# Attention beside a spectral mix: folded scans earlier, sums on another engine, two spectral blocks at another place

## The chip, the core and the metric

The kernel runs on one core of a Trainium2 chip. The time is the device time of one execution in microseconds (us), as the median of several runs. TensorE (PE) multiplies matrices into PSUM, VectorE (DVE) and ScalarE (ACT) read PSUM, GpSimd (POOL) works on SBUF, SyncE (SP) issues most transfers (DMAs). "PEld" in the profile is PE's loading of weights, which overlaps with its matmuls.

## What is computed

Two results over 2048 rows of 512 columns are mixed by a gate per row.

```python
g = sigmoid((x * gate_w).sum(-1, keepdims=True))
# a: attention, 32 heads of 16 columns
qkv = (x @ wqkv) split into q, k, v by heads
p = softmax(q k^T * 16**-0.5);  a = (p v, heads joined) @ wo
# b: spectral part, the real part of a transform along columns, then along rows
ar = x @ dft_hid_re^T;  ai = x @ dft_hid_im^T
b = dft_seq_re @ ar - dft_seq_im @ ai
out = g * a + (1 - g) * b
```

## The kernel before, in words

Most products are taken in three parts for precision: an operand is split into a high and a low part (`hi`, `lo`), and hi x hi, hi x lo and lo x hi are summed in PSUM. `halves_of` (L180) issues one such part as a pair of matmuls, one for each half of the rows, into two PSUM banks; the two halves are added afterwards. A pair is also called a slot, because `products` (L331) calls `beside()` (L284) after each pair, and `beside()` is where other work is interleaved by hand: it runs what `after(n, f)` had put down for n slots later (`run_due`), and issues scans at a pace.

A *scan* takes the scores of 128 queries with 512 keys for the two heads of a pair of heads, and from them the maximum that the softmax will subtract. There are 16 pairs of heads and 64 scans for each, 1024 in all (`TOTAL`). A *plain* scan (`scan`, L125) is a pair of matmuls into a tile of two banks and one DVE reduction of 128x1024. A *folded* scan (`scan_folded`, L140) compares keys two by two: ACT takes relu of the scores with the difference of two key blocks, DVE adds the scores of the second block and takes the maximum of the sums in the same instruction. It needs differences of keys in DRAM (`kf_d`), which `fold_keys` (L405) prepares out of stored keys, and single banks (`psk`: d0, d1, k0, k1) instead of the two-bank tiles of `pss1`.

The program has three stages.

1. The projections (L376 to L594): `project_t` for queries and keys (32 tiles of 12 slots, stored to DRAM), then `project_s` for values, real and imaginary spectral operands (48 tiles of 12 slots): 960 slots. In `project_s` ACT copies both halves out of PSUM (L472, L473), and POOL adds them four slots later (L544, L568). The sums for the spectral operands are stored to DRAM and loaded back, and ACT and POOL split them (`split_operand`, L348). Plain scans of the first three pairs of heads run beside this stage, one in 3.9 slots from slot 192 on.
2. The spectral blocks (L599 to L694): 24 of the 32 blocks of 48 slots (16 real, 8 imaginary), 1152 slots, with coefficients that POOL splits (`prepare`). Beside them run 500 folded scans, one in 2.19 slots. At the boundary of the stages the `pss1` banks are closed and `psk` is opened (L596).
3. The attention (L959): 512 steps, each with scores, exponentials on ACT (L233, L241) and products with values (L723, `pv`). The remaining scans go one to a step with plain reductions, 332 of them; from step `MIX` = 333 on, the 8 spectral blocks that are left (`LATER`, in `spectral`, L843) and then the output projection take that place, three pairs to a step.

`FRONT` = 564 + 16 x `LATER` is the number of scans ahead of stage 3. `load_scan_beside` (L276) loads the rows of the next pair of heads with eight DMAs from ACT's queue. `shift` (L162) works up the maxima of a finished pair on DVE. What orders the work is thus the order of the calls in the program; every engine executes its own instructions in that order, and waits by semaphores.

## Time and profile before

| | us |
|---|---|
| median of 3 runs | 1741.79 |
| lowest and highest of them | 1741.0, 1744.22 |
| the profiled execution | 1744.89 |
| its span, first to last instruction | 1743.1 |
| PE, DVE, ACT, POOL busy | 1716.2, 1159.3, 1451.3, 719.3 |

The views used below are: the page's head; busy time of each engine by stretch of the span ("PE busy (x)" is busy time and number of instructions, then the granted clock as a share of full speed, the busy share of the DMA engines and GB/s); groups of instructions by line and shape ("busy, mean ns of one | idle time before them, and what ended it"); waits ("engine, what waited <- what it waited for: us in total, times, longest"); and the timeline of an engine (start, duration, engine, line, operation, and in brackets the idle time before it and what ended it). A busy PE is not PE at its peak, since matmuls overlap.

### The profile page before, as it was taken

The numbers are of one execution on the slowest core, as the hardware profiler recorded it, in microseconds if no ns is written. First come the engines' busy times: TensorE is split into PE (matmuls) and PEld (weight loads), VectorE is DVE, ScalarE is ACT, GpSimd is POOL, SyncE is SP. The second block draws the span as 40 slices with busy tenths as digits, with TensorE's granted clock in tenths as the row PEclk, the third lists the DMA queues.
The fourth block names the chain that finished last, engine by engine and source line by source line (L and its number), as shares of the span: only waits on it lengthen the run. The fifth ranks groups of instructions, "written<-read, shape, count | busy, mean of one in ns | idle before, by whom it ended". The sixth has DMA issues, their size and how long they took to land.

```text
span 1743.1 us, 35510 instructions
## 1 busy us (share of the span) xinstructions
PE 1716.2 (98%) x13640; PEld 1030.2 (59%) x13640; DVE 1159.3 (67%) x1877; ACT 1451.3 (83%) x2383; POOL 719.3 (41%) x818
## 2 busy tenths in 40 slices
PE   8999999999999999999999999999999999999998
PEld 7997777888888887333333333333334555555554
DVE  6899998999999988666666666666663212222333
ACT  5445436888888888999999999999999888888885
POOL 3688668555556664132323223232332322322222
PEclk9999999999999999999999999999999999999999
DMA  7782767343345546432332513515313254255712
GB/s 257 257 296 75 219 187 235 112 122 114 100 152 150 145 134 112 85 65 55 63 62 56 96 29 78 81 24 98 77 36 73 68 115 91 68 139 133 184 36 100
DMA packets 126777, 199.54 MB, mean 114 GB/s; under 512 B 53984, under 2 KB 56528, under 8 KB 119696
## 3 DMA queue, kind: packets, MB, share of 16 engines
q1 hardware_dynamic: 84336, 161.02, 35.0%
q0 software_dynamic: 38496, 19.47, 5.2%
q10 hardware_dynamic: 3776, 16.78, 3.7%
q8 instruction: 107, 1.75, 0.4%
q14 instruction: 62, 0.51, 0.1%
HBM read 135.14 MB, written 62.66 MB: 113 GB/s over the span
## 4 chain that ended last, share of the span: by engine, by line
PE 82%; DVE 7%; DMA 5%; POOL 2%; issue 2%; ACT 1%; SPq 0%; DVEq 0%; POOLq 0%; ACTq 0%
PE pvb L723 27%; PE s L209 18%; PE xy L184 17%; PE s L184 8%; PE s L153 7%; DVE mx L136 5%; PE s L134 5%; DMA lc<-ob 1%; DMA fa<-ks_d 1%; DMA abr<-ab_d 1%; POOL s L274 1%; DMA kf_d<-fa 1%; DMA raws<-wqkv 0%; DMA ab_d<-ab 0%; DVE fold L159 0%
## 5 line engine op out<-in xcount | busy, mean ns | idle before, releaser
L136 DVE TENSOR_REDUCE mx<-s 128x2 f32<-128x1024 f32 x524 | 627.2, 1222 | 205.0 <-PE s L134 204.9
L233 ACT ACTIVATE eb<-s 128x1024 f32<-128x1024 f32 x512 | 578.0, 1129 | 55.2 <-PE s L209 55.1
L241 ACT ACTIVATE e<-s 128x512 f32<-128x512 f32 x1022 | 607.6, 705 | 1.1 <-PE s L209 1.1
L723 PE MATMUL pvb<-eb,va 128*17 128x512 f32 x2052 | 515.9, 597 | 0.0
L723 PE MATMUL pvb<-e,va 128*17 128x512 f32 x2044 | 515.0, 597 | 0.0
L209 PEld LDWEIGHTS s<-qs,ks 50*128 50x128 f32 x2048 | 211.8, 184 | 368.0 <-ACT eb L233 280.6
L209 PE MATMUL s<-qs,ks 50*128 50x512 f32 x2048 | 427.1, 436 | 0.0
L184 PE MATMUL xy<-b,c 64*128 64x512 f32 x2640 | 420.0, 392 | 0.3 <-ACT c L340 0.3
L159 DVE CUSTOM_DVE_ANT_0 fold<-s,fold 128x512 f32<-128x512 f32 x500 | 338.4, 690 | 35.8 <-PE s L153 17.6
L157 ACT ACTIVATE fold<-s 128x512 f32<-128x512 f32 x500 | 295.7, 602 | 69.7 <-PE s L153 42.5
L184 PEld LDWEIGHTS xy<-b,c 64*128 64x128 f32 x2640 | 297.7, 187 | 16.8 <-ACT c L340 0.6
L153 PE MATMUL s<-ks,qs 48*128 48x512 f32 x1000 | 230.0, 403 | 5.8 <-DVE mx L159 5.2
L134 PE MATMUL s<-ks,qs 48*128 48x512 f32 x1048 | 214.6, 396 | 6.0 <-DVE mx L136 5.8
L735 POOL DMA_DIRECT2D lc<-ob x124 | 62.9, 514 | 299.3 <-DVE ob L732 299.1
L723 PEld LDWEIGHTS pvb<-eb,va 128*17 128x17 f32 x2052 | 69.1, 95 | 190.1 <-issue 181.9
L153 PEld LDWEIGHTS s<-ks,qs 48*128 48x128 f32 x1000 | 125.2, 184 | 45.2 <-DVE mx L159 18.0
L742 POOL DMA_DIRECT2D r_d<-lc x31 | 18.1, 583 | 295.2 <-DVE lc L741 283.8
L372 POOL TENSOR_TENSOR c<-craw,c 128x512 fp32r<-128x512 f32 x92 | 120.5, 1310 | 7.4
L371 POOL CAST c<-craw 128x512 fp32r<-128x512 f32 x92 | 56.9, 619 | 137.8 <-PE xy L184 134.2
L134 PEld LDWEIGHTS s<-ks,qs 48*128 48x128 f32 x1048 | 102.9, 183 | 17.6 <-DVE mx L136 10.6
L184 PE MATMUL xy<-w,b 64*128 64x512 f32 x768 | 105.9, 393 | 2.4 <-ACT ty L473 2.2
L744 POOL DMA_DIRECT2D rb<-r_d x124 | 60.1, 493 | 70.5 <-DMA r_d<-lc 70.5
(130 smaller groups left out, 1511.9 us busy)
## 6 DMA issues: line engine op xcount, KB each, us to landing
craw<-ci SPq DMA_DIRECT2D x64, 256.0 KB
craw<-cr SPq DMA_DIRECT2D x60, 256.0 KB
ks<-k_d SPq DMA_DIRECT2D x46, 256.0 KB
qs<-q_d SPq DMA_DIRECT2D x46, 256.0 KB
ab_d<-ab SPq DMA_DIRECT2D x32, 256.0 KB
y_d<-y SPq DMA_DIRECT2D x32, 256.0 KB
o_d<-oh POOLq DMA_DIRECT2D x28, 256.0 KB, 9.9
o_d<-ol POOLq DMA_DIRECT2D x28, 256.0 KB, 11.7
```

The lines of the kernel that those rows point to most:

```text
L134: nc.tensor.matmul(ps[:, j, :], qs[b:b + 48, qb * P:(qb + 1) * P], ks[b:b + 48, c * 512:(c + 1) * 512], start=True, stop=True)
L136: nc.vector.tensor_reduce(mx[p][:, :, qb, c], ps, axis=AX.X, op=ALU.max)
L153: nc.tensor.matmul(ps, qs[b:b + 48, qb * P:(qb + 1) * P], ks[b:b + 48, c * 512:(c + 1) * 512], start=True, stop=True)
L157: nc.scalar.activation(fold[j], ps, AF.Relu)
L159: nc.vector.tensor_tensor_reduce(out=fold[j], in0=ps, in1=fold[j], scale=1.0, scalar=-3.0e38, op0=ALU.add, op1=ALU.max, accum_out=mx[p][:, ...
L184: nc.tensor.matmul(ps[j], lhs[r], rhs[r], start=first, stop=last)
L209: nc.tensor.matmul(pss[j], ks[b:b + 50, kb * P:(kb + 1) * P], qs[b:b + 50, q0:q0 + 512], start=True, stop=True)
L233: nc.scalar.activation(e, ps, AF.Exp, scale=SCALE)
L241: nc.scalar.activation(e[j], pss[j], AF.Exp, scale=SCALE)
L372: sub(lo, raw, hi.bitcast(F32))
L723: nc.tensor.matmul(pvb[r:r + VC, :], va[:, kb, 2 * p + j, :], es[c][j], start=kb == 0, stop=kb == NB - 1, tile_position=(0, r))
L735: nc.gpsimd.dma_start(lc[32 * n:32 * n + 32, :], ob[r + DH:r + VC, :].rearrange("p (s e) -> p s e", e=16))
```

## The change

Five things are changed.

- `LATER` is 10 instead of 8: two more of the imaginary spectral blocks are computed beside the attention, and 32 more scans ahead of it (`FRONT` 724 instead of 692, `MIX` 301 instead of 333).
- Scans are folded from the second pair of heads on. The change of banks moves from the boundary of the stages into the projections (`begin_folds`), the pace of folded scans is 2.67 slots there and 2.12 behind it (2.97 at two places). `scan_plain` goes.
- The pairs of heads are scanned in another order: 0, 4, 5, 6, 7, 1, 2, 3, 8, 9, then the first 20 scans of pair 11, then 10 (`SEQ`), and rows are loaded at other points (`ROWS`). For the heads 8 to 15 (the second block of 128 columns) the key differences are taken directly from the projected keys (`difference`); `fold_keys` is left for the first and the third block.
- In `project_s` ACT copies only one half, and DVE adds the other half directly from PSUM, three slots later, for values and for spectral operands.
- The program is built with a smaller scratch for the descriptors of dynamic DMAs.

```diff
-LATER = 8
+LATER = 10
-PACE = 3.9
-FOLDED = range(3 * SCANS, FRONT)
-FOLD_PACE = 2.19
-NARROW = 5.3
+FOLDED = range(SCANS, FRONT)
+PACE, BESIDE, PART, SWAP = 3.9, 2.67, 2.12, 2.97
+PART_PAIR = FRONT // SCANS
+EARLY = [0, 4, 5, 6, 7, 1, 2, 3, 8, 9]
+SEQ = [(p, i) for p in EARLY for i in range(SCANS)]
+SEQ += [(PART_PAIR, i) for i in range(FRONT % SCANS)] + [(p, i) for p in range(len(EARLY), PART_PAIR) for i in range(SCANS)]
+SEQ += [(n // SCANS, n % SCANS) for n in range(FRONT, TOTAL)]
+ROWS = {SCANS * n + (36 if n else 40): p for n, p in enumerate(EARLY[1:])}
+ROWS.update({SCANS * len(EARLY) - 54: PART_PAIR, SCANS * len(EARLY) - 24: len(EARLY)})
...
             def beside():
...
-                pace[1] += (PACE / FOLD_PACE if seen[0] in FOLDED else 1.0) / pace[0]
-                if seen[0] == FOLDED[0] and not beds:
-                    pace[1] = 0.0
+                pace[1] += 1.0 / pace[0]
...
-                    if n % SCANS == 36 and n - n % SCANS + SCANS < FRONT:
-                        load_scan_beside(n // SCANS + 1)
+                    if n == FOLDED.start:
+                        begin_folds()
+                    if n in ROWS:
+                        load_scan_beside(ROWS[n])
                     if n not in FOLDED:
-                        done = scan_plain(n)
+                        scan(n, s1())
+                        done = n
...
+            fp = pf.enter_context(tc.tile_pool(name="fp", bufs=2, reuse_waits="tile"))
+            banks = ExitStack()
+            pss1.append(banks.enter_context(tc.tile_pool(name="pss1", bufs=2, space=PSUM)))
+
+            def begin_folds():
+
+                banks.close()
+                psk.append(ctx.enter_context(tc.tile_pool(name="psk", bufs=1, space=PSUM, reuse_waits="tile")))
+                beds.extend((lambda tag: narrow(tag, "s"), fp))
+                scan_at(BESIDE)
...
+                def difference(f, c, s):
+
+                    kept.append(s)
+                    if c % 2 == 0:
+                        return
+                    a, b = kept
+                    kept.clear()
+                    hi = ep.tile([P, 512], F32R, tag="dh", name="dh")
+                    lo = a.bitcast(F32R)
...
+                    after(11, nc.gpsimd.tensor_sub, a, a, b)
+                    after(16, nc.scalar.copy, hi, a)
+                    after(17, nc.gpsimd.tensor_sub, lo, a, hi.bitcast(F32))
+                    after(22, store, 0, hi)
+                    after(25, store, 1, lo)
...
-                    if folded and 0 < f < ND - 1:
+                    if folded and f == 1:
+                        difference(f, c, s)
+                    if folded and f == 2:
                         after(10, nc.sync.dma_start, ks_d[f][:, c * 512:(c + 1) * 512], s)
...
-                    tx = ep.tile([P, 512], F32, tag="tx", name="tx", bufs=1)
-                    ty = ep.tile([P, 512], F32, tag="ty", name="ty", bufs=3)
+                    tx = ep.tile([P, 512], F32, tag="ty", name="tx", bufs=3)
                     nc.scalar.mul(tx, ps[0], sign)
-                    nc.scalar.mul(ty, ps[1], sign)
-                    after(4, use, t, tx, ty)
+                    after(3, use, t, tx, ps[1], nc.vector.tensor_add if sign > 0 else nc.vector.tensor_sub)
...
-                def to_values(t, tx, ty):
-                    nc.gpsimd.tensor_add(va[:, t, :, 0:DH], tx.rearrange("p (h e) -> p h e", e=DH),
-                                         ty.rearrange("p (h e) -> p h e", e=DH))
+                def to_values(t, tx, ps, add):
+                    add(va[:, t, :, 0:DH], tx.rearrange("p (h e) -> p h e", e=DH),
+                        ps.rearrange("p (h e) -> p h e", e=DH))
...
-                        nc.gpsimd.tensor_add(ab, tx, ty)
-                        after(7, nc.sync.dma_start, ab_d[i][t], ab)
+                        add(ab, tx, ps)
+                        after(5, nc.sync.dma_start, ab_d[i][t], ab)
...
-                for n, wait in enumerate((18, 78, 138, 170, 202, 234)):
-                    after(wait, fold_keys, *divmod(n, 2))
+                for n, wait in enumerate((18, 78, 138, 202)):
+                    after(wait, fold_keys, 2 * (n // 2), n % 2)
...
-                    if t == 12:
-                        scan_at(5.0)
...
-    nc = bacc.Bacc("TRN2", target_bir_lowering=False, num_devices=1)
+    nc = bacc.Bacc("TRN2", target_bir_lowering=False, num_devices=1, dynamic_dma_scratch_size=4096)
```

44 lines of the change are left out of this document (16 added, 28 removed).

## The prediction

> **What bounds the kernel now.** I first read the head of the page, for the span and the share of each engine.
>
> ```profile
> span 1743.1 us, 35510 instructions
> ...
> PE 1716.2 (98%) x13640; PEld 1030.2 (59%) x13640; DVE 1159.3 (67%) x1877; ACT 1451.3 (83%) x2383; POOL 719.3 (41%) x818
> ```
>
> TensorE (PE) looks full over the whole span, so the busy share alone tells nothing about which part could become shorter. Therefore I cut the span into stretches at the marks of the program (first scan, end of the projections, first attention step, first spectral block behind the scans) and read the busy times by stretch. The bracket behind each busy time counts instructions.
>
> ```profile
> core 0: us, PE busy (x) PEld busy (x) DVE busy (x) ACT busy (x) POOL busy (x), PEclk, DMA share, GB/s
> 56.80:113.10 56.30, 56.30 (x485) 56.02 (x481) 55.08 (x49) 27.87 (x51) 43.54 (x35) 1.00 0.77 265
> 142.70:170.60 27.90, 27.90 (x242) 22.62 (x240) 27.90 (x26) 14.57 (x34) 23.63 (x20) 1.00 0.26 76
> 170.60:289.60 119.00, 113.39 (x958) 88.97 (x957) 115.03 (x108) 49.67 (x95) 82.89 (x66) 1.00 0.74 218
> 289.60:691.90 402.30, 396.55 (x3314) 341.70 (x3312) 362.27 (x1046) 329.49 (x573) 230.14 (x226) 1.00 0.47 130
> 711.38:1263.16 551.78, 550.14 (x4063) 206.00 (x4061) 372.29 (x347) 550.43 (x871) 164.63 (x248) 1.00 0.35 65
> 1331.84:1594.08 262.24, 262.24 (x2164) 139.16 (x2160) 55.84 (x96) 233.91 (x362) 69.58 (x103) 1.00 0.43 104
> ```
>
> Four things are to be seen, and matmuls come in pairs throughout, one for each half of the rows.
>
> 1. In the first two rows PE issues 485 + 242 matmuls in 56.30 + 27.90 us, so a pair costs 84.2 / 363.5 = 0.2316 us when nothing holds PE up. This is the floor.
> 2. The third row, the end of the projections, has 958 matmuls, 479 pairs, which would take 110.9 us at the floor. It took 119.0, so 8.1 us were lost. The fourth row, the spectral blocks, has 1657 pairs or 383.8 us of floor in 402.3 us: 18.5 us lost. Projections and spectral blocks are thus bounded by PE, with a loss of 5 to 7%.
> 3. In the fifth row, the attention steps with a scan each, a step has 14 matmuls (4 scores, 2 scan, 8 values), so 4063 are 290 steps of 551.78 / 290 = 1.903 us. ScalarE (ACT) is busy for 550.43 of the 551.78 us: ACT sets this pace.
> 4. In the sixth row, the steps with spectral work, a step has 18 matmuls, 2164 are 120 steps of 262.24 / 120 = 2.185 us, and ACT is free for 28 us. PE sets this pace.
>
> **The change part by part.** *Two spectral blocks move.* A block is 48 pairs. The 32 scans that they push forward are 32 pairs. So 96 pairs leave the spectral stage and 32 enter the part ahead of the attention: 64 pairs fewer, 64 x 0.2316 = **-14.8 us** at an unchanged loss.
>
> In the attention, 32 steps change from the pace of the fifth row to that of the sixth: 32 x (2.185 - 1.903) = **+9.0 us**. The step at which the output rows begin is the same in both kernels (301 + 160 = 333 + 128 = 461), so what lies behind is unchanged. The additional coefficient splits on VectorE (DVE), loads and stores lie in a stretch where DVE is busy 55.84 of 262.24 us and cost nothing; without that cover, eight splits of two DVE instructions would stand there.
>
> [...] The fifth row shows PE 550.14 us busy of 551.78, as full as the sixth. Read by that, moved pairs cost in the attention what they save ahead of it, 14.8 us, and the gain is nil. [...]
>
> *Folded scans from the second pair on.* These rows give the price of a scan on its engines, and of the sums.
>
> ```profile
> L136 DVE TENSOR_REDUCE mx<-s 128x2 f32<-128x1024 f32 x524 | 627.2, 1222 | 205.0 <-PE s L134 204.9
> ...
> L159 DVE CUSTOM_DVE_ANT_0 fold<-s,fold 128x512 f32<-128x512 f32 x500 | 338.4, 690 | 35.8 <-PE s L153 17.6 <-ACT fold L157 6.3 <-POOL mx L150 1.3
> ...
> L157 ACT ACTIVATE fold<-s 128x512 f32<-128x512 f32 x500 | 295.7, 602 | 69.7 <-PE s L153 42.5 <-DVE mx L159 5.1
> ...
> L568 POOL TENSOR_TENSOR ab<-tx,ty 128x512 f32<-128x512 f32 x32 | 41.3, 1291 | 17.7 <-ACT ty L473 8.7 <-DMA ab_d<-ab 4.9 <-issue 2.3
> ...
> L274 DVE TENSOR_TENSOR s<-xy,tx 128x512 f32<-128x512 f32 x11 | 7.5, 683 | 5.9 <-ACT tx L446 5.8
> ```
>
> A plain scan is one reduction of 128x1024. In the second row of the stretches DVE is never idle while PE runs 121 pairs; with one scan per 3.9 slots (a slot is one pair of the projection) that is 121 / 4.9 = 24.7 scans, 1.13 us each. DVE and PE are both full there. A folded scan costs DVE 338.4 / 500 = 0.677 us and ACT 295.7 / 500 = 0.591 us.
>
> In the order of the changed kernel's instructions, folds begin at slot 445 of 960 instead of 963, 194 scans are folded within the projections, and 466 instead of 500 behind them. At one scan in 2.67 slots, 12 slots of a projection hold 4.49 scans, 16.5 pairs, 3.82 us of PE. DVE has 4.49 x 0.677 = 3.04 us of folds and one sum of 0.683 us (the last row has such a sum from PSUM), 3.72 us. It fits with 0.1 us to spare. ACT has 4.49 x 0.591 + 0.6 = 3.3 us, and some casts.
>
> What a folded scan costs PE by waiting is shown for the spectral stage, by the waits of PE's weight loads between 300 and 690 us:
>
> ```profile
> PEld s L153 <- DVE mx L159: 15.3, 49, 1.4
> PEld s L153 <- ACT fold L157: 6.7, 20, 0.8
> ```
>
> The 18.5 us of loss over 500 folds are 0.037 us a fold, all causes together. Behind the projections there are 34 folds fewer: **-1.3 us**, at a pace of 2.12 instead of 2.19 slots, which I count as nothing. Within the projections 194 folds cost between nothing (the plain scans of the second row lose nothing) and 194 x 0.037 = 7.2 us. The period is 3.67 x 0.2316 = 0.85 us there, not 0.74, so the slack over 0.677 us is three times as large; I take a third, **+2.4 us**. The change of PSUM banks from plain to folded scans comes once in either kernel, only earlier: nothing.
>
> *Sums on DVE.* From slot 384 to 445 five sums fall on DVE while scans are still plain. DVE then has 3.08 x 1.13 + 0.683 = 4.16 us for each 12 slots, which PE does in 15.1 x 0.2316 = 3.49: 0.67 us too much, five times, **+3.3 us**. I bound it by nothing below, since later slack can't return time that PE has lost but two banks may absorb part of it.
>
> On the other side the 48 sums leave GpSimd (POOL), each 1.29 us in the row of L568, and ACT evacuates one half instead of two. The waits between 170.6 and 300 us show what this stretch suffers from:
>
> ```profile
> ACT tx L472 <- POOL ab L568: 17.8, 11, 4.2
> ACT fh L274 <- POOL fa L274: 12.8, 5, 4.7
> POOL fa L274 <- DMA fa<-ks_d: 12.7, 4, 4.5
> ACT b L340 <- DMA abr<-ab_d: 10.0, 6, 2.5
> ...
> PEld s L134 <- DVE mx L136: 6.0, 8, 2.1
> ```
>
> ACT waited 17.8 us for POOL before it could reuse the buffer, and 12.8 us for folded keys that POOL had late because their loads came late (12.7). The change takes the first away, since the buffer now has three copies and no POOL sum behind it. It also takes away two of the three doublings of key folds: four folds at distances of 60, 60 and 64 slots are left where six stood, the last four 32 slots apart. I expect half of the 8.1 us of the third stretch back, **-4 us**, with bounds of nothing and 8.1.
>
> *Other edits, counted at nothing.* The direct difference of keys (two POOL subtractions of 1.29 us per 24 slots, a cast, two stores) lies between 70 and 90 us, where POOL is busy 43.54 of 56.30 us; uncovered it would be four times 2.6 us on POOL alone. The other order of pairs changes which rows are loaded, eight loads each on ACT's queue, 88 instead of 80. [...]
>
> ```profile
> 936.25 2.02 POOL L735 DMA_DIRECT2D lc<-ob  x4 [7.17 <-DVE ob L732]
> ...
> 958.68 0.82 POOL L758 DMA_DIRECT2D o_d<-ol  x1
> 966.54 2.02 POOL L735 DMA_DIRECT2D lc<-ob  x4 [7.05 <-DVE ob L732]
> ```
>
> POOL's chain for one half ends 7 us ahead of the next, so a few us more per half stay covered.
>
> *Sum.* -14.8 + 9.0 - 1.3 + 2.4 + 3.3 - 4 = **-5.4 us**, against the profiled execution's 1744.9 us (span 1743.1), whose time is 3.1 us above the median 1741.8. Carried over to the median: 1741.8 - 5.4 = **1736.4 us**.
>
> **The rivals.** (a) *DVE saturates in the projections.* If a fold there takes 0.73 us instead of 0.677, which the 0.69 us duration in its row makes possible with a gap, 12 slots need 4.49 x 0.73 + 0.683 = 3.96 us of DVE against 3.82 of PE. Over 43 such stretches that is +6 in place of +2.4, and the third stretch gives nothing back: -14.8 + 9.0 - 1.3 + 6 + 3.3 = +2.2, about 1743 us. For it speaks that DVE is the engine PE waits for in the rows above; against it, that the loss per fold is small even at 0.74 us.
>
> (b) *ACT's waits for transfers land on the scans; the side of slower.* ACT works in order. In the last projection it waits for reloaded operands:
>
> ```profile
> 255.41 0.54 SPq L345 DMA_DIRECT2D abr<-ab_d  x1
> ```
>
> ```profile
> 262.33 0.62 ACT L340 CAST b<-abr 128x512 fp32r<-128x512 f32 x1 [2.46 <-DMA abr<-ab_d]
> ```
>
> The load was issued at 255.41 and its cast began 2.46 us late. Together with the late key folds ACT waits 12.8 + 10.0 = 22.8 us in 11 waits. Now these hold up only evacuations with two banks of slack. After the change, evacuations of folded scans stand behind them on ACT's queue, and their PSUM bank is needed again after two scans, 2 x 0.85 us, less a matmul and an evacuation: about 0.6 us of slack. If all waits stay, 22.8 - 11 x 0.6 = 16 us fall on PE, of which some 3 are lost already: -14.8 + 9.0 - 1.3 + 2.4 + 3.3 + 13 = +11.6, 1753 us; if half stay, +5, 1747 us. It decides as soon as these waits exceed 0.6 us each. Against it: the loads get out earlier, because the store ahead of them on SP's queue no longer waits for POOL, and the key folds are half as dense.
>
> (c) *The projections lose nothing any more.* All 8.1 us come back, folds cost nothing there and the plain stretch is absorbed: -14.8 + 9.0 - 1.3 - 8.1 = -15.2, 1726.6 us; midway to the forecast about 1731.
>
> (d) *The blocks are simply moved.* If the pairs were paid in full in the attention (the reading by PE's busy time), the sum would be +0.4: 1742 us.
>
> **How the numbers follow.** Chances: the forecast 0.47, (a) 0.18, (b) 0.13, (c) 0.18, (d) 0.04. The range takes in the bounds: low -14 (short of (c)'s end) and high +4.7 (194 folds at 7.2, nothing back), or **1728 to 1746 us**. A measurement of this kernel can tell about 0.2% from no change, 3.5 us, so "faster" is below 1738.3 and "slower" above 1745.3. The forecast case spreads some 4 us around its middle: two thirds of it and all of (c) and a little of the others are faster, 0.55; slower is nearly all of (b) and a little of (a), 0.15; the rest is 0.30.
>
> **What would show each step.** The attention's steps: about 1.90 us up to step 300 and 2.185 from there, 32 more of the latter. The projections and spectral blocks together: the first score matmul about 14 us earlier than now, between 7 and 24 us. Per projection of 12 slots behind the start of the folds: 3.8 to 3.9 us; 4 us or more is (a). In the waits: ACT for POOL's sums gone; ACT for reloaded operands and key folds under 1 us each, otherwise (b), and then PE waits for ACT's folds. In the stretch with plain scans and sums: PE waits for reductions, 3 us in all. The prediction is wrong if steps with spectral work take other than 2.185 us, or if PE's loss before the attention changes by more than 8 us.

## The result, and the profile after

The changed kernel took 1769.1 us (median of 4 runs, 1765.0 to 1770.7) against 1741.9 us: 1.015 times the time before, interval 1.0131 to 1.017. The forecast was 1736.4 us. The execution that was profiled is the fastest of the four, 1765.0 us, so its trace can account for 19.7 us of span, from 1743.1 to 1762.8, of the 27.2 us between the medians.

The head of the page after:

```profile
span 1762.8 us, 36034 instructions
...
PE 1725.6 (98%) x13640; PEld 1029.4 (58%) x13640; DVE 1111.7 (63%) x2105; ACT 1510.0 (86%) x2491; POOL 638.7 (36%) x750
```

DVE and POOL have less to do, as planned, and ACT has more; PE has the same 13640 matmuls and needs 20 us more. As in the prediction, the stretches tell more. Here they are for the kernel after, cut at the same places of the program: slots 192 to 384, 384 to 442, 442 to 576, 576 to 960, the spectral stage, 290 attention steps, and 120 steps with spectral work.

```profile
core 0: us, PE busy (x) PEld busy (x) DVE busy (x) ACT busy (x) POOL busy (x), PEclk, DMA share, GB/s
54.67:117.07 62.40, 58.96 (x485) 47.88 (x482) 55.53 (x49) 29.04 (x53) 48.53 (x39) 0.97 0.69 237
117.07:136.61 19.54, 18.39 (x147) 13.27 (x148) 18.55 (x19) 5.73 (x12) 9.99 (x8) 1.00 0.97 307
136.61:184.57 47.96, 45.85 (x370) 35.59 (x367) 41.82 (x112) 40.87 (x86) 20.37 (x16) 1.00 0.28 79
184.57:320.59 136.02, 131.68 (x1058) 105.39 (x1056) 118.75 (x335) 108.52 (x204) 34.82 (x27) 1.00 0.59 181
320.59:698.13 377.54, 369.97 (x3058) 321.05 (x3057) 335.19 (x988) 307.87 (x537) 208.55 (x205) 0.99 0.48 129
717.08:1274.22 557.14, 550.73 (x4062) 203.64 (x4062) 372.99 (x346) 551.46 (x871) 167.17 (x250) 1.00 0.32 59
1351.33:1613.79 262.46, 262.46 (x2165) 139.31 (x2161) 55.72 (x96) 233.97 (x362) 71.15 (x107) 1.00 0.41 101
```

Two stretches of the kernel before that the prediction did not show, slots 384 to 442 and 442 to 576, are needed beside them:

```profile
113.12:130.74 17.62, 17.40 (x149) 13.82 (x148) 17.20 (x16) 7.79 (x16) 14.04 (x12) 1.00 0.94 304
130.74:170.64 39.90, 39.69 (x338) 31.50 (x336) 39.87 (x40) 20.69 (x48) 33.23 (x27) 1.00 0.27 74
```

A loss is, throughout, the length of a stretch less 0.2316 us for each pair of matmuls in it. In slots 576 to 960, for instance, 136.02 - 529 x 0.2316 = 13.5 us.

| part | lost before | lost after | more | forecast |
|---|---|---|---|---|
| slots 0 to 192 (the head; 51.0 us long, then 48.9) | | | -2.2 | 0 |
| 192 to 384 (keys, plain scans) | 0.2 | 6.2 | +6.0 | 0 |
| 384 to 442 (sums beside plain scans) | 0.4 | 2.5 | +2.1 | +3.3 |
| 442 to 960 (sums and folds) | 8.8 | 18.6 | +9.8 | +2.4 - 4 |
| spectral stage | 18.5 | 23.4 | +4.9 | -1.3 |
| 64 pairs fewer ahead of the attention | | | -14.8 | -14.8 |
| attention | | | +14.0 | +9.0 |

These add up to 19.8 us. The head's -2.2 us is mostly not the change's: the profiled execution before has a stretch at half the clock there (at 37.6 us, see the last section), the one after has none, and neither has e3 below, which has the head of the kernel before and takes 49.2 us for it. The attention is taken from the first value matmul (692.4 us before, 698.1 after) to the last matmul. Its last row above is as forecast, 262.46 us for 120 steps, 2.187 a step; the row ahead of it is not, 557.14 us for 290 steps that took 551.78.

The groups that changed:

```profile
L141 DVE TENSOR_REDUCE mx<-s 128x2 f32<-128x1024 f32 x364 | 441.3, 1224 | 186.0 <-PE s L139 186.0
...
L164 DVE CUSTOM_DVE_ANT_0 fold<-s,fold 128x512 f32<-128x512 f32 x660 | 442.8, 690 | 51.9 <-PE s L158 22.1 <-ACT fold L162 10.6 <-PE xy L189 1.8
...
L592 DVE TENSOR_TENSOR ab<-tx,xy 128x512 f32<-128x512 f32 x32 | 22.0, 686 | 6.7 <-ACT tx L497 6.0 <-issue 0.3
```

A fold still takes 0.69 us and a sum on DVE 0.686 us. The prices of the single operations were right; what failed is what they cost when they stand in each other's way. The timeline shows four places. First the key projection of the second block, where `difference` was added:

```profile
93.55 1.30 POOL L279 TENSOR_TENSOR s<-s,dh 128x512 fp32r<-128x512 f32 x1
...
94.80 1.27 POOL L279 TENSOR_TENSOR s<-s,tx 128x512 f32<-128x512 f32 x1
96.10 0.62 ACT L279 CAST eh<-s 128x512 fp32r<-128x512 f32 x1 [3.10 <-POOL s L279]
...
97.10 0.59 ACT L474 COPY s<-xy 128x512 f32<-128x512 f32 x1
97.74 0.30 PEld L189 LDWEIGHTS xy<-b,c 64*128 64x128 f32 x4 [3.16 <-ACT s L474]
```

POOL runs one operation of 1.3 us after the other, here the low part of the difference ahead of the sum of the next tile. ACT's cast waits 3.10 us for that sum, ACT's copies out of PSUM stand behind the cast, and PE waits 3.16 us for a copy. The second place, in the spectral stage:

```profile
546.47 4.52 SPq L678 DMA_DIRECT2D early<-ab_d  x8
...
550.63 0.32 ACTq L104 DMA_DIRECT2D qs<-q_d  x1
551.05 1.78 ACT L162 ACTIVATE fold<-s 128x512 f32<-128x512 f32 x3 [3.67 <-DMA early<-ab_d]
551.69 0.69 DVE L164 CUSTOM_DVE_ANT_0 fold<-s,fold 128x512 f32<-128x512 f32 x1 [3.57 <-ACT fold L162]
551.71 0.50 PE L158 MATMUL s<-ks,qs 48*128 48x512 f32 x2 [3.19 <-ACT fold L162]
```

SP issues eight loads in 4.52 us; a load of scan rows that ACT has to issue in its order gets out only at 550.63, and ACT's folds behind it wait 3.67 us. The third, in the attention:

```profile
804.18 0.25 DVE L759 RECIPROCAL lc<-lc 128x16 f32<-128x16 f32 x1 [2.50 <-DMA lc<-ob]
804.35 1.16 DVE L141 TENSOR_REDUCE mx<-s 128x2 f32<-128x1024 f32 x1
...
805.56 0.50 PE L139 MATMUL s<-ks,qs 48*128 48x512 f32 x2 [1.63 <-DVE mx L141]
```

The reciprocal for the division by the row sums waits 2.50 us in DVE's order for its transfer, the scan's reduction stands behind it, and PE waits for that. DVE's waits for this transfer up to 1300 us, before and then after, are:

```profile
DVE lc L741 <- DMA lc<-ob: 4.4, 5, 1.9
```

```profile
DVE lc L759 <- DMA lc<-ob: 20.6, 11, 7.1
```

The fourth place is no single one. From 137 to 321 us PE's weight loads wait for the folds' banks:

```profile
PEld s L158 <- DVE mx L164: 15.4, 32, 1.1
PEld s L158 <- ACT fold L162: 4.1, 10, 1.0
```

### The profile page after: what moved, and what is told of

It is laid out like the page before. It is cut to its first block, busy times and chain, and to the rows that moved or that the text cites. A ratio compares the mean times of both kernels' runs of the same rounds, so it can differ in the third digit from the quotient of the medians.

```text
span 1762.8 us, 36034 instructions
## 1 busy us (share of the span) xinstructions
PE 1725.6 (98%) x13640; PEld 1029.4 (58%) x13640; DVE 1111.7 (63%) x2105; ACT 1510.0 (86%) x2491; POOL 638.7 (36%) x750
## 4 chain that ended last, share of the span: by engine, by line
PE 81%; DMA 6%; DVE 5%; POOL 3%; issue 2%; ACT 2%; SPq 0%; DVEq 0%; ACTq 0%; POOLq 0%
PE pvb L741 25%; PE xy L189 19%; PE s L214 16%; PE s L189 9%; PE s L158 9%; DMA lc<-ob 4%; PE s L139 4%; DVE mx L141 2%; DVE fold L164 1%; POOL s L279 1%; POOL el L279 1%; ACT fold L162 1%; POOL lc L753 1%; ACT tx L497 0%; ACT eh L279 0%
## 5 line engine op out<-in xcount | busy, mean ns | idle before, releaser
L141 DVE TENSOR_REDUCE mx<-s 128x2 f32<-128x1024 f32 x364 | 441.3, 1224 | 186.0 <-PE s L139 186.0
L164 DVE CUSTOM_DVE_ANT_0 fold<-s,fold 128x512 f32<-128x512 f32 x660 | 442.8, 690 | 51.9 <-PE s L158 22.1
L162 ACT ACTIVATE fold<-s 128x512 f32<-128x512 f32 x660 | 388.3, 602 | 98.6 <-PE s L158 66.4
L189 PE MATMUL xy<-b,c 64*128 64x512 f32 x2448 | 398.7, 396 | 3.1 <-ACT s L474 3.0
L158 PE MATMUL s<-ks,qs 48*128 48x512 f32 x1320 | 324.7, 409 | 14.0 <-DVE mx L164 8.3
L189 PEld LDWEIGHTS xy<-b,c 64*128 64x128 f32 x2448 | 281.8, 189 | 23.7 <-ACT s L474 4.3
L158 PEld LDWEIGHTS s<-ks,qs 48*128 48x128 f32 x1320 | 175.7, 185 | 70.8 <-DVE mx L164 29.7
L139 PE MATMUL s<-ks,qs 48*128 48x512 f32 x728 | 153.7, 398 | 7.8 <-DVE mx L141 7.3
L189 PE MATMUL xy<-w,b 64*128 64x512 f32 x768 | 119.4, 393 | 0.3 <-ACT s L474 0.2
L189 PE MATMUL s<-b,chi 64*128 64x512 f32 x670 | 105.3, 390 | 0.3 <-ACT chi L1054 0.3
L189 PEld LDWEIGHTS xy<-w,b 64*128 64x128 f32 x768 | 84.2, 186 | 12.7 <-ACT s L474 1.1
## 6 DMA issues: line engine op xcount, KB each, us to landing
o_d<-oh POOLq DMA_DIRECT2D x28, 256.0 KB, 10.4
```

Of the source, the lines that this page charges most:

```text
L139: nc.tensor.matmul(ps[:, j, :], qs[b:b + 48, qb * P:(qb + 1) * P], ks[b:b + 48, c * 512:(c + 1) * 512], start=True, stop=True)
L141: nc.vector.tensor_reduce(mx[p][:, :, qb, c], ps, axis=AX.X, op=ALU.max)
L158: nc.tensor.matmul(ps, qs[b:b + 48, qb * P:(qb + 1) * P], ks[b:b + 48, c * 512:(c + 1) * 512], start=True, stop=True)
L162: nc.scalar.activation(fold[j], ps, AF.Relu)
L164: nc.vector.tensor_tensor_reduce(out=fold[j], in0=ps, in1=fold[j], scale=1.0, scalar=-3.0e38, op0=ALU.add, op1=ALU.max, accum_out=mx[p][:, ...
L189: nc.tensor.matmul(ps[j], lhs[r], rhs[r], start=first, stop=last)
```

## The experiments

The theories at the start were: (T1) in the projections an operation more on DVE or ACT, the two engines that empty the folds' banks, is longer than the slack that is left, so sums beside folds at this pace cost about 9 us; (T2) three long single waits, with what follows them, cost about 10 us ahead of the attention and 5 in it; against these (R1) the smaller scratch slows transfers, and (R2) the blocks cost in the attention all that they save ahead of it. For T1, the stretch from slot 442 to 912 is the one to look at. Before and after:

```profile
130.74:274.60 143.86, 139.70 (x1182) 110.09 (x1180) 141.49 (x133) 61.91 (x127) 103.02 (x82) 1.00 0.60 172
```

```profile
136.61:302.12 165.51, 160.62 (x1294) 128.10 (x1292) 144.62 (x403) 134.28 (x261) 49.98 (x39) 1.00 0.48 147
```

The loss is 143.86 - 591 x 0.2316 = 7.0 us before and 165.51 - 647 x 0.2316 = 15.7 us after. (The expectations say 16.0, 13.7, 6.7 and 2.9 us where such rows give 15.7, 13.2, 6.4 and 2.7: they were counted in the trace by single starts of matmuls.) Each such number is from one execution. Five more kernels, e2, e4, e5, e8 and e10, have the changed kernel's code in this stretch, and their traces give the same loss within 0.2 us; e15, which has e9's code there, loses 6.5 us where e9 loses 2.7.

**e1_pool_sums: the sums back on POOL, the rest of the change kept.**

```diff
+ty = ep.tile([P, 512], F32, tag="ty", name="ty", bufs=3)
 nc.scalar.mul(tx, ps[0], sign)
-after(3, use, t, tx, ps[1], nc.vector.tensor_add if sign > 0 else nc.vector.tensor_sub)
+nc.scalar.mul(ty, ps[1], sign)
+after(4, use, t, tx, ty, nc.gpsimd.tensor_add)
```

> The changed kernel with the sums of the projections as before: ACT copies both halves, POOL adds them; all else as changed. Theory 1 (a sum on DVE delays the folds behind it, each fold's bank is single, and PE waits in order): the loss between slots 442 and 912, 16.0 us above the floor of 0.2316 us a pair, falls to about 7, and the 2.6 us between slots 384 and 442 to under 1; the time falls from 1769 to about 1758 us. Theory 2 (folded scans lose this much beside projections by themselves, because of ACT's casts and the pace): the loss stays within 3 us of 16, the time is 1766 to 1772 us.

1773.3 us, ratio 1.0174 (1.0161 to 1.0188).

```profile
134.04:302.36 168.32, 160.49 (x1294) 127.95 (x1291) 124.01 (x364) 150.68 (x300) 100.52 (x79) 1.00 0.48 144
```

The loss is 168.32 - 149.9 = 18.5 us, not less. So it is not that DVE has the sums: with a second copy on ACT it is as bad. But ACT is now busy for 150.68 us, more than the 149.9 us that PE would take, and PE's weight loads wait 17.7 us for ACT's folds and 3.3 us for DVE's. The theory as first put fell; what stays is that both engines empty banks, and that this run fills the other one.

**e2_later8: eight blocks behind the scans, the rest of the change kept.**

```diff
-LATER = 10
+LATER = 8
-ROWS.update({SCANS * len(EARLY) - 54: PART_PAIR, SCANS * len(EARLY) - 24: len(EARLY)})
+ROWS[SCANS * len(EARLY) - 54] = PART_PAIR
```

> The changed kernel with the two spectral blocks and their 32 scans left where they were (LATER = 8); all else as changed, the same paces. If the move is worth what the prediction said (64 pairs of 0.2316 us saved against 32 steps of 0.282 us), this is 5.8 us slower than the changed kernel, about 1775 us, and its attention has 332 steps of 1.90 us. If moved pairs cost in the attention what they save ahead of it, it is 1769 us; if the attention's late transfers (5 us in the changed kernel's profile) come with the moved blocks, 1770 us.

1771.0 us, ratio 1.0164 (1.015 to 1.0178). The attention, from the first value matmul on, takes 1042.2 us instead of 1057.3, and all ahead of it ends 21.3 us later (719.4 us instead of 698.1). By the medians the moved blocks are worth 1.9 us (1771.0 against 1769.1), which is less than either kernel's runs are apart; by the two traces they are worth 6.2 us. So R2 is near in its result, and wrong in its reason: 9 of the 15 us are the pace of the steps, as forecast; the rest are waits for the late transfer, which are 1.3 us in this run. On the other side the 21.3 us hold, beside the 14.8 us of the pairs, a wait of 5.5 us at the end of the stage that the changed kernel hasn't.

**e3_before_scratch: the kernel before with the smaller scratch alone.**

```diff
-nc = bacc.Bacc("TRN2", target_bir_lowering=False, num_devices=1)
+nc = bacc.Bacc("TRN2", target_bir_lowering=False, num_devices=1, dynamic_dma_scratch_size=4096)
```

> The kernel before, built with the smaller scratch for dynamic DMAs, nothing else. Theory A (the smaller scratch makes the row sums' transfers from POOL land later, and DVE, which waits for them, holds up a scan): waits of DVE for these transfers rise from 13 us towards 29, the time rises by about 5 us to 1747. Theory B (the scratch does nothing, the attention's late transfers come from something else): 1742 us, within 2 us, and waits of about 13 us.

1741.4 us, ratio 0.9995 (0.9986 to 1.0004). R1 falls, for the kernel before.

**e4_stalls: a first attempt on the single waits.**

```diff
+ROWS[460] = ROWS.pop(484)
-nc.gpsimd.memset(mx[p], -3.0e38)
+nc.vector.memset(mx[p], -3.0e38)
-load_w(wv, wqkv[:, 1024:1536], 48, nc.gpsimd)
+load_w(wv, wqkv[:, 1024:1536], 60, nc.gpsimd, 20)
```

(The last argument is the distance of the four splits, 24 before.)

> The changed kernel with three single stalls taken away: the splits of the value weights on POOL come 12 slots later and 20 instead of 24 apart, the rows of the pair that were loaded together with eight operand loads (scan 484) are loaded at scan 460, and the maxima of the part pair are cleared by DVE instead of POOL. Theory 3 (these stalls of 3.1, 3.6 and 1.3 us are lost on PE, and each of the two long ones costs another 1.7 us because the granted clock is halved for 3.4 us behind it): 11 us less, 1758 us, and two half-clock stretches fewer. Rival (PE has the time elsewhere, or the stalls move to the next wait): 1765 us or more.

1767.9 us, ratio 1.0152 (1.0138 to 1.0166). Only the wait behind the memset went. At 95.8 us PE still stood 3.2 us, so the split of weights in POOL's queue was not what made POOL late; and the loads that meet the burst are those of scan 548, not 484. Both were misread from the timeline.

**e5_stalls2: the same with the right places.** To the memset and the splits of e4 come:

```diff
+ROWS[524] = ROWS.pop(548)
-after(11, nc.gpsimd.tensor_sub, a, a, b)
-after(16, nc.scalar.copy, hi, a)
+after(9, nc.gpsimd.tensor_sub, a, a, b)
+after(14, nc.scalar.copy, hi, a)
```

> The changed kernel with its single long waits of TensorE taken apart: the splits of the value weights on GpSimd come later and closer together; the rows of pair 9 are loaded at scan 524 instead of 548, away from the loads that fill the queue at 548 us; the key difference's subtraction and cast come two slots sooner; the -3e38 memset goes from GpSimd to VectorE. Theory of single waits (the gaps of 3.1, 3.6 and 1.3 us and the two half-clock stretches of 1.7 us lost behind the first two make a tenth of the loss each): -3.1 - 1.7 - 3.6 - 1.7 - 1.3 = -11 us, about 1758. Rival (the waits are taken by the next thing that is late, or the loss is spread over the folds): 1765 or more.

1759.3 us, ratio 1.0102 (1.0088 to 1.0116): 9.8 us less, 11 expected. The 48 slots around the burst, 21.53 us long in the changed kernel, take 16.49:

```profile
543.20:559.69 16.49, 16.49 (x143) 15.28 (x141) 14.87 (x46) 13.81 (x26) 8.94 (x9) 1.00 0.61 213
```

In the key projection two shorter waits are left of the long one, 1.1 and 1.4 us. T2 holds for the two places.

**e6_split_sums: each sum on DVE in two halves.**

```diff
-add(ab, tx, ps)
-after(5, nc.sync.dma_start, ab_d[i][t], ab)
+for n in range(2):
+    c = slice(256 * n, 256 * n + 256)
+    after(3 * n, add, ab[:, c], tx[:, c], ps[:, c])
+after(7, nc.sync.dma_start, ab_d[i][t], ab)
```

> The changed kernel with each VectorE sum cut in two halves of 256 columns, three slots apart, the second store two slots later. Theory of the bank slack (a sum of 0.68 us in VectorE's order is longer than the about 0.5 us by which a fold may be late before TensorE waits for its bank): the loss from slot 442 to 912 falls from 16 us to 8 to 10, total about 1762. Rival (the mean load of the engines or ScalarE's casts decide): the loss stays at 14 or more, 1766 to 1772.

1770.3 us, ratio 1.0163 (1.0149 to 1.0176).

```profile
138.74:300.92 162.18, 159.12 (x1294) 130.69 (x1292) 144.27 (x443) 134.68 (x261) 49.67 (x39) 1.00 0.49 148
```

The loss is 12.3 us, between theory and rival: 3.4 us less, where 6 to 8 were expected. The total did not follow, since single waits elsewhere differed.

**e7_no_sums: no sum at all** (this kernel leaves out the second half's product from the values and the spectral operands).

```diff
-add(ab, tx, ps)
+nc.gpsimd.tensor_copy(ab, tx)
```

(and the same for the values)

> The changed kernel without the sums of the two halves in the projections with a sign (GpSimd copies the first half only, so the values and the spectral operands lack the second half's product; all matmuls, loads and stores stay). VectorE then has nothing but scans there, ScalarE one copy. Theory of the bank slack: the loss from slot 384 to 442 falls under 1 us, and from 442 to 912 to about 7, total about 1758. Rival (the folds themselves at this pace, ScalarE's casts or the loads make the loss): the loss from 442 to 912 stays over 13, total 1765 or more.

1758.2 us, ratio 1.0091 (1.0077 to 1.0105).

```profile
135.93:294.00 158.07, 155.64 (x1293) 130.92 (x1291) 124.21 (x364) 133.65 (x261) 72.78 (x78) 1.00 0.51 153
```

The loss is 158.07 - 149.7 = 8.3 us; from slot 384 to 442 it is 0.7. So the sums cost 15.7 - 8.3 = 7.4 us here, and folds at this pace without them little more than plain scans and POOL's sums did (7.0).

**e8_divide_later: the division two attention steps later.**

```diff
-halved.append((step + (7 if done[0] < NP - 1 else 3), quotients(*done[:2])))
+halved.append((step + (9 if done[0] < NP - 1 else 3), quotients(*done[:2])))
```

> The changed kernel with the division by the row sums two attention steps later (9 instead of 7 after the last value matmul), so that VectorE's reciprocal doesn't stand waiting for its transfer in front of a scan. Theory of the late transfer: the bumps at 803, 835, 927, 1051 and 1252 us go, the attention takes 1052 us instead of 1057, total about 1764. Rival (the bumps are bandwidth that the attention needs anyway): no change, 1769.

1760.1 us, ratio 1.0102 (1.0087 to 1.0118). The same 290 steps:

```profile
718.83:1269.63 550.80, 550.08 (x4062) 207.68 (x4062) 373.55 (x346) 550.13 (x871) 164.43 (x248) 1.00 0.30 60
```

That is 1.899 us a step, and the attention takes 1050.8 us instead of 1057.3. Why the transfer comes later in the changed kernel, and only with ten blocks behind the scans, was not shown.

**e10_stalls_divide: e5 and e8 in one.**

```diff
+ROWS[524] = ROWS.pop(548)
...
+after(9, nc.gpsimd.tensor_sub, a, a, b)
...
+halved.append((step + (9 if done[0] < NP - 1 else 3), quotients(*done[:2])))
```

> The edits of the two runs before in one kernel: the single waits taken apart (1759.3 us alone) and the division two steps later (attention 6.5 us shorter alone). If they lie in different stages and add: 1769.1 - 9.8 - 6.5 = about 1753 us. Rival (the long waits move elsewhere, as the half-clock stretches do): 1757 or more.

1752.1 us, ratio 1.0058 (1.0045 to 1.0071). They add.

**e11_all: further, e6's halves, plain-scan sums on POOL, and the boundary's operand splits on POOL.**

```diff
+if beds:
     after(3, use, t, tx, ps[1], nc.vector.tensor_add if sign > 0 else nc.vector.tensor_sub)
+else:
+    ty = ep.tile([P, 512], F32, tag="tx", name="ty", bufs=1)
+    nc.scalar.mul(ty, ps[1], sign)
+    after(4, use, t, tx, ty, nc.gpsimd.tensor_add)
...
-after(4 + 6 * d, split_operand, NB - 4 + d, tail[:, d, :], nc.vector if d < 2 else nc.gpsimd)
+after(4 + 6 * d, split_operand, NB - 4 + d, tail[:, d, :], nc.gpsimd)
```

> As the run with both edits, and further: sums in two halves once folds run, sums by two ScalarE copies and GpSimd while scans are plain, and the first two operand splits at the change of stage on GpSimd instead of VectorE. Theory of the bank slack: 3.3 us less from slot 442 to 912 (measured in the run with split sums), 2 us less from 384 to 442, 3 to 5 us less at slot 960: 1743 to 1746 us. Rival (GpSimd is late with the operands, or the gains don't add): 1750 or more.

1744.1 us, ratio 1.001 (1.0001 to 1.0018), 25 us below the changed kernel. From slot 442 to 912:

```profile
133.65:296.82 163.17, 159.31 (x1295) 129.66 (x1292) 143.62 (x440) 135.20 (x263) 52.10 (x41) 1.00 0.49 151
```

13.2 us are still lost here.

**e9_all_later8: e11 with eight blocks behind, and folds at one scan in 3.6 slots.**

```diff
-LATER = 10
+LATER = 8
-PACE, BESIDE, PART, SWAP = 3.9, 2.67, 2.12, 2.97
+PACE, BESIDE, PART, SWAP = 3.9, 3.6, 2.2, 2.97
```

(and `ROWS` as in e2)

> As the run with all edits, but eight blocks behind the scans as in the kernel before, so that the projections' folds come at one scan in 3.6 slots instead of 2.67. The blocks moved back cost 14.8 - 9.0 = 5.8 us. If the mean load of the engines beside the folds makes the loss, it falls from about 12 to 6 us between slot 442 and 912, and the total is the same as with all edits or 2 us less. If each sum's collision with a fold makes it, the loss stays over 10 and the total is 5 us above the run with all edits.

1741.7 us, ratio 0.9997 (0.9988 to 1.0006).

```profile
135.71:277.49 141.78, 141.25 (x1201) 115.63 (x1199) 115.93 (x347) 110.29 (x217) 52.18 (x41) 1.00 0.56 169
```

141.78 - 600.5 x 0.2316 = 2.7 us are lost. With the same sums at the same places, a slower pace of the folds takes most of the loss away. The total is that of the kernel before.

**e12_before_sums: the kernel before with DVE's sums alone** (`project_s`, `to_values` and `to_rhs` as in the change).

```diff
-nc.scalar.mul(ty, ps[1], sign)
-after(4, use, t, tx, ty)
+after(3, use, t, tx, ps[1], nc.vector.tensor_add if sign > 0 else nc.vector.tensor_sub)
```

> The kernel before with nothing but the sums taken by VectorE from PSUM, beside plain scans to the end of the projections. By the term of the prediction a projection of 12 slots beside plain scans then has 4.16 us of VectorE against 3.49 us of TensorE: 48 times 0.67 = 32 us more, less at most 8 us that the third stretch had lost: 1766 to 1774 us. Rival (two banks absorb the sums): 1745 or less.

1762.8 us, ratio 1.0119 (1.0106 to 1.0133).

```profile
132.14:294.50 162.36, 150.29 (x1182) 105.70 (x1180) 162.22 (x171) 43.27 (x89) 55.05 (x43) 1.00 0.53 157
```

DVE is busy for 162.22 of 162.36 us: beside plain scans it is the bound, and the prediction's term has the right mechanism. Its size was too large: the attention begins 19.1 us later than before, 0.40 us for each of the 48 projections, not 0.67, and the total is 3 us below the range expected. Beside plain scans at this pace the sums on DVE cost more than they save.

**e13_alternate: e11 with every second sum by ACT and POOL.**

```diff
-if beds:
+if beds and t % 2:
```

> As the run with all edits (ten blocks behind the scans), but every second projection of the later half has its sum from two ScalarE copies and GpSimd, so that the load of the sums is shared: per 12 slots 3.04 + 0.34 = 3.38 us for VectorE and 2.65 + 0.9 = 3.55 us and casts for ScalarE, against 3.82 us of TensorE. Theory of the mean load: the loss from slot 442 to 912 falls from 13.7 to 8 us or less, total 1738 to 1740 us. Rival (ScalarE is then as full as VectorE was): 1744 or more.

1753.7 us, ratio 1.0073 (1.0059 to 1.0087).

```profile
133.20:301.84 168.64, 162.52 (x1292) 126.59 (x1290) 133.92 (x402) 142.57 (x281) 77.99 (x74) 1.00 0.47 146
```

The loss rises to 168.64 - 149.6 = 19.0 us, although DVE has 9.7 us less to do than in e11 and ACT 7.4 us more. The gain that the theory of the mean load had forecast did not come, and the rival's time did (1744 or more): ACT, busy for 142.57 us, is now as full as DVE was in e11 with 143.62. So this run doesn't refute that the fuller engine decides. PE's waits for ACT's folds rose from 7.6 to 12.0 us; those for DVE's did not fall, 9.2 and 10.4.

**e14_alternate_later8: the same alternation on e9.**

```diff
-if beds:
+if beds and t % 2:
```

> The same alternation on the run with eight blocks behind the scans and folds at one scan in 3.6 slots. VectorE and ScalarE have slack there already (a loss of 2.9 us from slot 442 to 912), so by the theory of the mean load little is left to gain: 1740 to 1742 us, a loss of 2 to 3 us. By the theory of single collisions half of that loss goes.

1741.1 us, ratio 1.0001 (0.9992 to 1.001).

```profile
134.31:277.30 142.99, 141.99 (x1202) 119.56 (x1200) 105.39 (x309) 119.03 (x236) 77.78 (x74) 1.00 0.54 165
```

The loss is 142.99 - 601 x 0.2316 = 3.8 us: nothing to gain at the slower pace.

**e16_even_pace: e11 with another spacing of the same folds.**

```diff
-PACE, BESIDE, PART, SWAP = 3.9, 2.67, 2.12, 2.97
+PACE, BESIDE, PART, SWAP = 3.9, 2.9, 2.05, 2.97
```

> The run with all edits (ten blocks behind the scans) with one scan in 2.9 instead of 2.67 slots beside the projections and one in 2.05 instead of 2.12 beside the spectral blocks: nothing but the spacing of the folds changes. A scan's period in the projections grows from 3.67 to 3.9 slots (0.85 to 0.90 us). Theory of the slack of one period against one extra operation (0.6 to 0.7 us): the loss from slot 442 to 912 falls from 13.7 to about 9 us, the one from 1008 to 1584 rises from 6.0 by 2 to 4: total 1740 to 1743 us. Rival (the number of sums and folds decides, not their spacing): 13 us or more in the first, total 1745 or more.

1741.6 us, ratio 0.9998 (0.9989 to 1.0007).

```profile
134.14:287.14 153.00, 150.99 (x1266) 127.27 (x1263) 135.24 (x412) 127.26 (x249) 52.24 (x41) 1.00 0.49 156
```

153.00 - 633 x 0.2316 = 6.4 us, half of e11's 13.2. The folds are the same, but with the wider spacing 14 fewer scans fall into this stretch. In the spectral stage the loss between slots 1008 and 1584 rose from 6.0 to 8.4 us, as expected, and behind slot 1632 from about 5 to about 10, which was not.

**e15_rows_back: e9 with the rows of pair 9 loaded at scan 548 again.**

```diff
-ROWS[524] = ROWS.pop(548)
```

> The run with all edits and eight blocks behind the scans, with the rows of pair 9 loaded at scan 548 again: with this spacing of scans it was scan 524 whose loads met the eight loads of the filled queue at 511 us (a wait of 1.9 us of ScalarE's folds and 1.5 and 1.1 us of TensorE). If the meeting of the two bursts is what costs, 1.5 to 2.5 us go: about 1739.5. Rival (another pair's loads meet them, or the later burst meets the end of the stage): 1742 or more.

1744.0 us, ratio 1.001 (0.9999 to 1.0021). PE's wait at the burst only went from 1.5 to 1.2 us, and other waits appeared at 210 and 984 us. It tells nothing for the theory. But up to slot 912 this kernel has the code of e9, and yet it loses 6.5 us from slot 442 on, with a wait of PE of 1.7 us and 3.4 us at half the clock behind it: so far can two executions differ.

**e17_renew_pool: e16 with 8 of 16 operand subtractions on POOL instead of 4.**

```diff
-after(4, (nc.gpsimd if s % 4 == 3 else nc.vector).tensor_sub, al[s], raw, ah[s].bitcast(F32))
+after(4, (nc.gpsimd if s % 2 else nc.vector).tensor_sub, al[s], raw, ah[s].bitcast(F32))
```

> The run with the even pace, and at the change from one half of the spectral operands to the other every second instead of every fourth subtraction on GpSimd (two more of VectorE's eight... sixteen in all). In the run before, a subtraction of VectorE took 1.2 to 1.8 us there and TensorE waited 1.8 and 1.2 us behind two of them. If VectorE's load at this place is the cause, the loss behind slot 1632 falls from 10.5 to about 7 us: 1738 us. Rival (GpSimd then is late with the coefficients that the matmuls need): 1741 or more.

1738.5 us (1736.6 to 1740.0, 11 runs), ratio 0.998 (0.9972 to 0.9989). From slot 1632 to the end of the stage, in e16 and then here:

```profile
544.97:681.99 137.02, 133.03 (x1096) 112.59 (x1093) 123.68 (x348) 110.76 (x195) 79.14 (x75) 1.00 0.52 137
```

```profile
542.78:677.21 134.43, 132.06 (x1095) 113.63 (x1093) 119.13 (x344) 110.90 (x195) 83.76 (x79) 1.00 0.54 140
```

2.6 us of it are gone. This kernel has the idea of the change, ten blocks behind the scans, and is 0.2% faster than the kernel before.

**e18_pace_285: e17 at 2.8 and 2.08 slots.**

> As the run beside it, with a pace of 2.8 and 2.08 slots, halfway between the two spacings tried. By the slack of a period the loss from slot 442 to 912 lies between 6.7 and 13.7 us, at about 9, and the spectral stage loses 1 us less than with the even pace: 1739 to 1741 us. Rival (there is a threshold above the length of one extra operation): 7 or less in the projections.

1739.7 us, ratio 0.9991 (0.9982 to 1.0).

```profile
133.53:287.94 154.41, 152.89 (x1275) 131.96 (x1273) 137.41 (x424) 130.30 (x254) 52.34 (x41) 1.00 0.49 155
```

154.41 - 637.5 x 0.2316 = 6.8 us, nearly as at 2.9 slots (6.4). So the loss falls steeply between 2.67 and 2.8 slots and hardly from there to 2.9, which is for the rival; with one execution for each pace, a step is likely and not proven.

## Why the prediction was wrong

*What was right.* The floor of 0.2316 us, the 64 pairs fewer, the steps of 2.185 us (2.187) and of 1.903 (1.899 once the late transfer is out of the way, e8), the mechanism of the sums beside plain scans (+3.3 forecast, 2.1 measured; e12), and nothing for the scratch (e3, 1741.4 us). That PE's busy share does not tell what bounds the steps ahead of step 300 can be read in the prediction's rows: PE is busy for 550.14 of 551.78 us there and for all of 262.24 us behind, yet it starts 7.4 matmuls per us (4063) against 8.3 (2164), while ACT is busy for 550.43 us. The waits that "-4" was to remove did go: from 137 to 321 us ACT waits for no POOL sum and for no load, so the waits that rival (b) named are gone too.

That moving two blocks pays is not shown. With all the other edits, ten blocks behind the scans (e16, 1741.6 us) and eight (e9, 1741.7 us, with other paces) take the same time. That e17 ends 2.1 us from the forecast comes from edits that the prediction does not have; for the forecast it is luck.

*The step that failed most: sums beside folds, put at nothing.* The prediction has "+3.3" for five sums beside plain scans, "+2.4" for 194 folds and "-4" for the stalls that go. The 43 sums beside folds have no term, since DVE's 3.72 us in 12 slots fit into 3.82 us of PE "with 0.1 us to spare". For slots 442 to 960 that makes 1.6 us less; measured are 9.8 us more. The load was forecast well: DVE is busy for 144.62 us where PE's floor is 149.9, 0.97 of it, as 3.72 is of 3.82. What failed is that a mean load of 0.97 costs nothing. Without the sums (e7) the loss from slot 442 to 912 falls from 15.7 to 8.3 us, so the sums cost 7.4 us there. With the sums and fewer folds beside them it falls to 6.4 us (e16) and 2.7 (e9), and with halved sums to 12.3 (e6). The prediction's own slack says why this may be: it was worked out for a period of 0.85 us with a fold alone, 0.677 us, while in a period with a sum DVE has 0.677 + 0.683 = 1.36 us to do. That the next folds' banks then come free too late is argued from this; no run isolates it.

The "-4" does not show either: even without sums (e7), 8.3 us are lost where the kernel before lost 7.0, so what the stalls may have returned, the folds took.

A folded scan passes both engines: ACT's output goes into DVE's fold, and PE waits for either to empty a bank. The table shows, from slot 442 to 912, the busy us of DVE plus ACT as a share of twice the floor of PE in the same stretch, and the fuller of the two engines as a share of the floor:

| | DVE + ACT | of twice the floor | fuller engine | lost, us |
|---|---|---|---|---|
| e14, alternating, 3.6 slots | 224.4 | 0.81 | ACT 0.86 | 3.8 |
| e9, 3.6 slots | 226.2 | 0.81 | DVE 0.83 | 2.7 |
| e7, no sums, 2.67 | 257.9 | 0.86 | ACT 0.89 | 8.3 |
| e16, 2.9 | 262.5 | 0.90 | DVE 0.92 | 6.4 |
| e18, 2.8 | 267.7 | 0.91 | DVE 0.93 | 6.8 |
| e1, sums by ACT and POOL, 2.67 | 274.7 | 0.92 | ACT 1.01 | 18.5 |
| e13, alternating, 2.67 | 276.5 | 0.92 | ACT 0.95 | 19.0 |
| the changed kernel, 2.67 | 278.9 | 0.93 | DVE 0.97 | 15.7 |
| e6, halves, 2.67 | 279.0 | 0.93 | DVE 0.96 | 12.3 |
| e11, halves, 2.67 | 278.8 | 0.93 | DVE 0.96 | 13.2 |

Up to 0.91 of both together, or 0.93 of the fuller one, the loss is at most 8.3 us; from 0.92, or 0.95, on it is 12 or more. Whether the joint load or the fuller engine alone decides stays open, because the two columns part the rows at the same place: e1 and e13 take load off DVE and make ACT as full as DVE had been. Within the lower group neither column orders the losses.

Rival (a), that a fold takes more of DVE than assumed, named the right sign and the right place ("4 us or more" for 12 slots: the 384 slots of the row from 184.57 us took 136.02 / 32 = 4.25). Its cause did not come: it had a fold at 0.73 us, and a fold took 442.8 / 660 = 0.671. Its price was +6 where +9.8 were measured, and DVE stayed below PE's floor.

Two slips in the prediction's sums change nothing of this: (a)'s +2.2 leads to 1744.0 us, not 1743, and the upper bound of +4.7 leaves out the -1.3, with which it is +3.4.

*"Counted at nothing": the key difference.* The cover was a mean, POOL busy 43.54 of 56.30 us. Within 24 slots the two subtractions come on top of four other operations and a split of weights: from 89.79 to 96.07 us POOL runs five operations of 1.3 us without a break, and PE's next tile waits for POOL through ACT's order. It cost 6.0 us with what follows a long wait, and e5's edits returned about half of it.

*"Counted at nothing": the order of pairs and their loads.* ACT issues them in its order, ahead of folds. One meeting with a burst on SP's queue cost 5 us in the spectral stage, and e5 removed it. That is rival (b)'s mechanism, ACT's in-order wait, at another transfer than the one it named.

*The attention's additional 5 us.* "The additional coefficient splits, loads and stores ... cost nothing" looked at DVE's busy share behind step 300. What was late lies ahead of it: a transfer for which DVE waits in order (4.4 us before, 20.6 after); e8 returned 6.5 us, and with it the attention takes 7.5 us more than before, near the +9.0.

*What the prediction had no row for* is what follows a wait: three stretches at half the clock, of some 1.6 us each, below.

## What to carry to other kernels

When work is moved onto engines that empty single buffers for another engine, a mean load that just fits is no cover: here 0.93 of the pace on the fuller engine (0.91 on both) went with a loss of 7 us, and 0.95 to 1.01 (0.92 to 0.93) with 12 to 19. Look at the one period that holds the additional operation, too. A cover is read at the place and in the order of the engine's queue, not from a mean over 50 us, and a DMA that an in-order engine issues is an instruction that can block (here ACT's folds waited 3.67 us behind one). After a move, look first for the few longest waits and spread the load again: e17 is the same idea with some distances and owners of small operations changed, and 30 us faster than the change as it came.

## What the hardware did that was not expected

**Half the clock after a wait.** Two stretches of the changed kernel, the wait in the key projection and what follows it:

```profile
95.00:98.00 3.00, 0.28 (x4) 0.26 (x4) 1.31 (x2) 1.59 (x3) 2.27 (x2) 1.00 0.40 143
98.83:102.24 3.41, 3.41 (x20) 2.66 (x18) 1.93 (x2) 2.11 (x4) 2.68 (x3) 0.50 0.88 332
```

PE was busy for 0.28 of 3 us; then the granted clock was 0.50 for 3.41 us, in which pairs of matmuls start 0.43 us apart instead of 0.23. Added up, each such stretch costs about 1.6 us, and the kernel after has three ahead of the attention (98.8, 327.5 and 552.8 us), the kernel before one (37.6 us). In each of the four the granted clock was 0.50 for 3.4 us. PE stood idle for 2.72 us ahead of the stretch above, and in e7 for 1.60 us, up to 796.03 us, with 0.50 from 796.5 us on. Yet the kernel before stood idle for 1.61 and 1.66 us, up to 187.56 and 280.82 us, and its clock was 1.00 in the 3.9 us behind either wait. So the length of a single wait doesn't decide alone; what else does was not shown.

**DVE slower beside POOL.** The subtractions of DVE, of which e17 moved four, in e16 (durations in ns, least, median and longest):

```profile
L280 DVE TENSOR_TENSOR b<-early,b x6: 684/930/1372, 557.0 to 573.2; 128x512 fp32r<-128x512 f32 x6
L280 DVE TENSOR_TENSOR b<-abr,b x6: 689/1454/1790, 573.8 to 591.9; 128x512 fp32r<-128x512 f32 x6
```

The same instruction takes 0.68 to 1.79 us, and at 573.81, where it took 1.79, POOL ran a sum of 1.83 us from 573.22 on. The trace shows the pattern in all twelve: the three that started with no POOL operation under way took 0.68 to 0.69 us, and the other nine ended 0.54 to 0.56 us behind the end of the POOL operation that was under way. The twelve of the changed kernel, from 577.51 to 608.38 us, show it too: five that started with no POOL operation under way took 0.68 to 0.69 us, and the other seven, of 0.69 to 1.50 us, ended 0.54 to 0.56 us behind the end of one. Folds and sums, which read one operand from PSUM, keep means of 0.69 us (the groups above). What makes the one end behind the other was not shown.
